# Weight steps of a gated FFN at fixed ticks of the attention in front of it

## The chip, the cores and the metric

The kernel runs on one core of a Trainium2 chip. Its time is the device time of one execution in microseconds (us). A core has a TensorE for matmuls (PE in the profile; PEld is its weight load), VectorE (DVE), ScalarE (ACT), GpSimd (POOL) and SyncE (SP), which here only issues transfers. Each engine works through its own instructions in order, and waits on semaphores for the others. TensorE accumulates in PSUM banks of 512 floats per partition.

## The reference

```python
def _attn_ref(q, k, v, s):                     # q, k, v: 8 x 8 x 576 x 64, s: 8 x 8 x 576
    scores = scale * np.matmul(q, k.transpose(0, 1, 3, 2))
    s_pos = np.maximum(s, 0.0)
    cum = np.cumsum(s_pos, axis=-1)
    bias = -(cum[:, :, :, None] - cum[:, :, None, :])
    scores = np.where(causal, -1000000000.0, scores + np.minimum(bias, 0.0))
    attn = np.exp(scores - np.max(scores, axis=-1, keepdims=True))
    attn = attn / (np.sum(attn, axis=-1, keepdims=True) + 1e-09)
    return np.matmul(attn, v)

def _moe_ref(x, w_gate, w_val, w_out):         # x: 4608 x 512, w: 512 x 1536 twice, 1536 x 512
    gate = 1.0 / (1.0 + np.exp(-(x @ w_gate)))
    return (gate * (x @ w_val)) @ w_out
```

Causal attention over 64 heads of 576 rows, and then a gated FFN over the 4608 rows that it gives. The three FFN weights are drawn in such a way that they reach the kernel as 64-bit floats.

## The kernel before

**Attention by ticks.** A head's 576 rows are five tiles (`TILES`): one of 64 rows and four of 128, with 64 to 576 columns, the widest first. The main loop runs over ticks `n`: one tick is one tile of one head, so head `i` has ticks 5i to 5i + 4. A tick issues the scores of tile n (`n_s` for the first eight heads in float32, `s_part` for the others in pairs of float16), and masks, minimum and exponential of the tile before it (`n_max`, `max_part`, lines 610 and 497). Twice in a head `p_part` (line 499) makes float16 pairs of the exponentials and sends them through a transposing transfer into `PT` (two buffers each). Two heads later `av_part` (line 519) multiplies them by v into the PSUM bank `av_bank`, `x_part` normalizes, and every second head `split_x` writes a slot of `xslots` that the FFN reads. There are ten slots, of which the last three are only made by `late_slots`.

**The weights.** There are 18 pieces (`wsteps`, line 230): twelve of the gate and value weights, one for each f of 12, and six of the output weight, each of 128 x 1024 numbers in 64 bits. Piece n is loaded in two halves of 512 KB (`load_weight`), the first two by SP, the others by ScalarE's queue, into one of six raw buffers; two of these lie in the room of the finished output weights (`w2room`), three in `t2big`, where the FFN keeps the results of its first 24 units (`t2first`). `weight_step` number n asks for loads up to n + 3, if the buffer's last user is two steps back; it decodes piece n (`decode_weight`: a ScalarE pass at line 266, a VectorE pass at line 268, then `square_rows`, a Gram matrix of eight matmuls at line 279 in the last 128 columns of `av_bank`, and its row maxima at line 283); and it finishes piece n - 1 (`split_weight`: a bound from the maxima by a matmul at line 288, a power-of-two scale from it, and the high and low float16 parts by ScalarE at line 308 and VectorE at line 309). So there are 19 steps, 0 to 18, with 18 of each kind of work.

**The FFN by units.** A unit (g, f) is a group of 256 rows and one f of 12: `ffn_in` with 24 matmuls (line 680; 48 smaller ones where a group spans two batches), a tanh (685), a VectorE product (687), the float16 pair of the result (`ffn_mid`, 695 and 696), and later `ffn_out` with six matmuls of 512 columns (710). There are 216 units. The first 24 (groups 0 and 1, batch 0) start at tick 44, and draw on the weights as these are made: `weights_through` runs the weight steps that a unit needs. Their `ffn_out` follows when all 24 are in and `hidden_scale` has the weights' scales. From then on units are spread over the ticks by `want`.

**v's scale.** `v_square` loads a batch's v (four loads of 288 KB) and `v_square_sum` squares and sums it on ScalarE; `v_scale` makes the scale. For batch 2 the loads go to free slots of `xslots`.

**What sets the order.** A scheduler orders each engine's instructions by program order and priority, with a model of their times; `first()` raises a priority. It may move an instruction ahead of others or behind them, as far as data and buffers allow. Accesses to one PSUM bank keep the order of the program. `tc.keep_in_program_order` holds an instruction in its place; `tc.issue_after(ins)` puts the instructions of its block, on the engine of `ins`, behind `ins`.

Before the change the steps are called so: `while n < NE and wnext["step"] < min(2 + n // 6, 9)` (steps 0 and 1 at tick 0, then one each six ticks, step 8 at tick 42), and from tick 45 on by the units through `weights_through`: step 9 at tick 45, and the other nine at ticks 50 to 55. The units come by `FPT` = 0.6 of two a tick and all 24 are issued by tick 63.

Of the kernel before, what the change touches and what calls it, by code (L numbers as in the profile page):

```python
# [25 lines left out]
def tile_attention_then_gated_ffn(  # L26
# [129 lines left out]
    def v_square(b, c):  # L156
        if c == 0:
            vss[b] = wp.tile([P, vch], F32, tag="vss", name=f"vss{b}")
        if b < 2:
            t = wp.tile([P, S], F32, tag="rl", name=f"vsq{b}_{c}")  # L160
        elif b == 2:
            t = xslots[NX - 1 - c].rearrange("p l n -> p (l n)").bitcast(F32)[:, :S]
        else:
            t = spare[f"vsq{c % 2}"]
        (nc.gpsimd if b < 2 else nc.sync).dma_start(t, vview[b, c])
        if b == 0:
            nc.scalar.activation(t, t, AF.Square, accum_out=vss[b][:, c : c + 1])
        else:
            vsq[b, c] = t
# [89 lines left out]
    def decode_weight(n):  # L259

        r = raw[wsteps[n][2]]
        if not wide:
            return r[:, : 8 * P].bitcast(F32)
        a = tops[n % 2]
        top = a.bitcast(F16).rearrange("p (n t) -> p n t", t=2)[:, :, 1]
        nc.scalar.activation(top, r.bitcast(BF16)[:, 4:].rearrange("p (n t) -> p n t", t=4)[:, :, 0], AF.Copy)
        v_ = r[:, : 16 * P].rearrange("p (n t) -> p n t", t=2)[:, :, 1]
        nc.vector.scalar_tensor_tensor(v_, v_, 13, a, ALU.logical_shift_right, ALU.bitwise_or)
        square_rows(n, a)
        return v_.bitcast(F32)  # L270

    wrow, wlast = {}, {}

    def square_rows(n, a):

        top = a.bitcast(BF16).rearrange("p (n t) -> p n t", t=2)[:, :, 1]
        ps = av_bank[:, 3 * P :]
        for c in range(8):
            ins = nc.tensor.matmul(ps, top[:, c * P : (c + 1) * P], top[:, c * P : (c + 1) * P],
                                   start=c == 0, stop=c == 7)  # L280
        wlast["gram"] = ins.ins
        wrow[n] = wp.tile([P, 1], BF16, tag="wss", name=f"wrow{n}")
        nc.vector.tensor_scalar(junk16, ps, 0.0, None, ALU.max, ALU.max, accum_out=wrow[n])
# [64 lines left out]
    def weights_through(n):  # L348
        while wnext["step"] <= n + 1:
            weight_step()  # L350
# [110 lines left out]
    def s_part(i, t):  # L461
        w = TILES[t][2]
        c0 = S + t * P - PAD
        lhs = T[i].rearrange("p a n -> p (a n)")[:, c0 : c0 + P]
        pieces = [(0, w)] if w <= 512 else [(0, w // 2), (w // 2, w)]
        S_ps[i, t] = []
        for a, b_ in pieces:
            ps = score_bank(f"s{i}_{t}_{a}")
            nc.tensor.matmul(ps[:, : b_ - a], lhs, T[i][:, 0, a:b_], start=True, stop=False)  # L469
            nc.tensor.matmul(ps[:, : b_ - a], lhs, T[i][:, 2, a:b_], start=False, stop=True)  # L470
            S_ps[i, t].append((ps, a, b_))

    def bias_row(i):
# [14 lines left out]
    def max_part(i, t):  # L488
        w = TILES[t][2]
        c = qkc[i // 2][1][:, 2:3]  # L490
        init = MASKED
        for n, (ps, a, b_) in enumerate(S_ps.pop((i, t))):
            acc = wp.tile([P, 1], F32, tag=f"em{n}", name=f"em{i}_{t}_{n}", bufs=3)
            nc.vector.tensor_tensor_reduce(e_t[t][:, a:b_], ps[:, : b_ - a], rl[i][:, a:b_], c, init,  # L494
                                           ALU.add, ALU.min, acc)
            init = acc
        nc.scalar.activation(e_t[t][:, :w], e_t[t][:, :w], AF.Exp, bias=init, scale=-1.0)  # L497

    def p_part(i, h_):

# [91 lines left out]
    def n_s(i, t):  # L592
        q0, m, w = TILES[t]
        p, j = divmod(i, 2)
        nS[i, t] = []
        for a, b_ in [(0, w)] if w <= 512 else [(0, w // 2), (w // 2, w)]:
            ps = score_bank(f"s{i}_{t}_{a}")
            nc.tensor.matmul(ps[:, : b_ - a], qT[i][:, q0 : q0 + P], kT[p][:, a:b_], start=True, stop=True)
            nS[i, t].append((ps, a, b_))

    def n_max(i, t):
        q0, m, w = TILES[t]
        init = MASKED
        r = rl[i]
        for n, (ps, a, b_) in enumerate(nS.pop((i, t))):
            acc = wp.tile([P, 1], F32, tag=f"em{n}", name=f"em{i}_{t}_{n}", bufs=3)
            nc.vector.tensor_tensor_reduce(e_t[t][:m, a:b_], ps[:m, : b_ - a], r[:m, a:b_], -1.0, init,
                                           ALU.add, ALU.min, acc[:m])
            init = acc[:m]
        nc.scalar.activation(e_t[t][:m, :w], e_t[t][:m, :w], AF.Exp, bias=init, scale=-1.0)  # L610

    def n_turn(i, t):

# [143 lines left out]
    NE, NOFF = 44, 87  # L757
    FPT = 0.6
    EARLY = 18
    VSQ = 66  # L760
    WLA = 3
    nticks = NTL * NH
    for n in range(nticks + 12):
# [43 lines left out]
        if i < NH:  # L807
# [74 lines left out]
            if b == 0:  # L882
                if t == 2 and 1 <= h < 1 + vch:
                    v_square(1, h - 1)
                if t == 4 and 1 <= h < 1 + vch:
                    v_square_sum(1, h - 1)
                if t == 1 and h == 6:
                    v_scale(1)
            elif b == 1:
                if VSQ <= n < VSQ + vch:  # L890
                    v_square(2, n - VSQ)
                if VSQ + 5 <= n < VSQ + 5 + vch:
                    c = VSQ + 4 + vch - n
                    v_square_sum(2, c)
                if n == VSQ + 11:
                    v_scale(2)
            elif b + 1 < B:
                if t == 0 and 2 <= h < 2 + vch:
                    v_square(b + 1, h - 2)
                if t == 4 and 2 <= h < 2 + vch:  # L900
                    v_square_sum(b + 1, h - 2)
                if t == 4 and h == 2 + vch:
                    v_scale(b + 1)
            while n < NE and wnext["step"] < min(2 + n // 6, 9):
                weight_step()

        if n >= NE and state["u"] < 2 * NF:
            fdone = min(NF, int((n - NE + 1) * FPT))
            while state["u"] < 2 * fdone:
                f = state["u"]  # L910
                if f == 0:
                    weights_through(gate_step[7])
                if f < NF and f % WLA == 0:
                    weights_through(gate_step[f + WLA - 1])
                    inverse_weights(0, slice(f, f + WLA))
                    ffn_scale(0, slice(f, f + WLA))
                if f >= NF:
                    weights_through(min(gate_step[NF - 1] + 2 * (f - NF + 1), len(wsteps) - 1))
                emit_unit()
            if state["u"] == 2 * NF:  # L920
                hidden_scale()
                while state["o"] < 2 * NF:
                    emit_out()
                late_slots()
# [45 lines left out]
```

## Time and profile before

| | |
|---|---|
| median of 3 runs | 1177.1 us (1176.61 to 1182.89) |
| the profiled execution | 1178.93 us |
| its span, first to last instruction | 1177.2 us |
| mean granted TensorE clock | 0.976 |
| PE busy | 1115.4 us (95%) |
| DVE busy | 755.2 us (64%) |
| ACT busy | 736.2 us (63%) |
| transfers | 157.65 MB, mean 134 GB/s |

The columns of a group row are: line, engine, operation, output and input with shapes, count; busy time in us and mean ns of one; idle time of the engine just before, and what ended it. A timeline row has start and length in us, then the same, with the wait before it in brackets. ACTq and SPq are the queues on which ScalarE and SyncE issue transfers. A row of stages has the stage, its length, busy time and count of each engine, the granted TensorE clock, the mean busy share of the 16 DMA engines and GB/s.

### The profile page before, as it was taken

To read this page: it belongs to the slowest core of one execution; us is meant where nothing else is said; L and a number is where in the kernel's file an instruction comes from. 1 tells how busy PE (TensorE), PEld (TensorE's weight loads), DVE (VectorE), ACT (ScalarE), POOL (GpSimd) and SP (SyncE) were. 2 spreads that over 40 slices of the span, in tenths; PEclk is the share of its full clock that TensorE was granted. 3 is DMA by queue.
4 is the path that set the end of the run, shared out by engine and by line. 5 is a ranking of instruction groups with operands and counts; after the bars stand their busy time and mean duration, and the time that the engine had idled before them with its cause. 6 is when DMAs were issued, how large, how long until landed. Compare 5 with 4: busy or idle time off the path is not lost.

```text
span 1177.2 us, 30611 instructions
## 1 busy us (share of the span) xinstructions
PE 1115.4 (95%) x11806; PEld 865.2 (73%) x11806; DVE 755.2 (64%) x2395; ACT 736.2 (63%) x1429; POOL 235.3 (20%) x553
## 2 busy tenths in 40 slices
PE   6898588799899999999999999999999999999998
PEld 4686477655777788778777777778877887787775
DVE  4667875887679777775656577777777775222222
ACT  4888664757678687776656577667776765233222
POOL 4423220223123222221111122212222221000000
PEclk8999798999999999999999999999999999999999
DMA  8877965999889899897565669878979774000000
GB/s 199 224 186 168 185 121 120 172 174 192 143 171 175 150 193 169 149 157 143 110 113 121 124 121 174 167 148 167 158 152 159 142 123 99 12 19 16 4 19 19
DMA packets 445520, 157.65 MB, mean 134 GB/s; under 512 B 403583, under 2 KB 435839, under 8 KB 445374
## 3 DMA queue, kind: packets, MB, share of 16 engines
q1 hardware_dynamic: 418686, 127.38, 59.3%
q10 hardware_dynamic: 23328, 17.04, 5.2%
q0 software_dynamic: 3360, 11.27, 2.9%
q8 instruction: 92, 1.51, 0.5%
q14 instruction: 54, 0.44, 0.1%
HBM read 56.92 MB, written 9.58 MB: 56 GB/s over the span
## 4 chain that ended last, share of the span: by engine, by line
PE 72%; DMA 10%; issue 6%; DVE 3%; ACT 3%; SPq 2%; POOL 2%; ACTq 0%; POOLq 0%; DVEq 0%
PE gv L680 41%; PE o L710 21%; PE s L470 3%; PE s L469 3%; DMA pt<-p 2%; PE av_bank L531 1%; PE av_bank L529 1%; PE av_bank L530 1%; DMA T<-qk 1%; DMA T<-T 1%; DMA ws<-in_moe_w_out_dram 1%; DMA v<-in_v_dram 1%; DMA w2all<-in_moe_w_out_dram 1%; POOL rl L484 1%; DMA cr<-cum_d 1%
## 5 line engine op out<-in xcount | busy, mean ns | idle before, releaser
L680 PE MATMUL gv<-x,w 128*128 128x256 f16 (+3 forms) x6912 | 621.5, 248 | 8.5 <-DVE t2f L687 7.2
L680 PEld LDWEIGHTS <-w 128*128 128x128 f16 x6912 | 539.0, 99 | 70.9 <-issue 6.4
L710 PE MATMUL o<-w2all,h 128*128 128x512 f16 x1296 | 321.6, 382 | 0.4 <-ACT io L729 0.4
L484 POOL TENSOR_SCALAR_AFFINE_SELECT rl<-rl 128x64 f32<-128x64 f32 (+1 forms) x280 | 107.8, 386 | 559.8 <-DVE em L494 495.0
L497 ACT ACTIVATE e<-e,em 128x576 f32<-128x576 f32 x280 | 154.1, 554 | 101.2 <-DVE em L494 98.1
L685 ACT ACTIVATE th<-gv,scb 128x256 f32<-128x256 f32 (+3 forms) x288 | 111.6, 413 | 154.1 <-PE gv L680 151.9
L710 PEld LDWEIGHTS <-h 128*128 128x128 f16 x1296 | 121.1, 96 | 112.3 <-issue 0.5
L687 DVE SCALAR_TENSOR_TENSOR t<-th,gv 128x256 f32<-128x256 f32 x192 | 80.1, 417 | 133.4 <-ACT th L685 130.6
L494 DVE CUSTOM_DVE_ANT_0 e<-s,rl,qkcf 128x288 f32<-128x288 f32 x280 | 135.8, 486 | 32.0 <-PE s L470 27.1
L695 ACT ACTIVATE h<-t,hsc 128x256 f16<-128x256 f32 x192 | 96.7, 503 | 78.9 <-DVE t L687 78.0
L506 DVE SCALAR_TENSOR_TENSOR p<-e,p 128x384 f16<-128x384 f32 x224 | 103.6, 502 | 47.9 <-ACT p L501 46.8
L696 DVE SCALAR_TENSOR_TENSOR h<-t,hsc,h 128x256 f16<-128x256 f32 x192 | 93.2, 485 | 45.1 <-ACT h L695 44.4
L501 ACT ACTIVATE p<-e 128x1152 f16<-128x1152 f32 x112 | 112.0, 1000 | 9.4 <-DMA pt<-p 7.0
L470 PE MATMUL s<-T 128*128 128x288 f16 (+2 forms) x246 | 62.7, 283 | 13.1 <-DMA T<-T 13.1
L469 PE MATMUL s<-T 128*128 128x288 f16 (+2 forms) x246 | 64.6, 281 | 5.7 <-DVE em L494 5.0
L529 PE MATMUL av_bank<-v,pt 128*128 128x65 f16 x560 | 67.9, 193 | 0.2 <-DVE xe_w L129 0.2
L531 PE MATMUL av_bank<-v,pt 128*128 128x65 f16 x560 | 68.1, 195 | 0.0
L530 PE MATMUL av_bank<-v,pt 128*128 128x64 f16 x560 | 68.0, 192 | 0.0
L432 POOL PARTITION_BROADCAST cr<-cr x63 | 57.5, 912 | 11.5 <-DMA cr<-cum_d 11.4
L529 PEld LDWEIGHTS <-pt 128*128 128x128 f16 x560 | 52.6, 98 | 6.1 <-issue 1.1
L530 PEld LDWEIGHTS <-pt 128*128 128x128 f16 x560 | 52.6, 97 | 5.5 <-issue 0.3
L478 DVE TENSOR_SCALAR rl<-cr,qkcf 128x576 f32<-128x576 f32 x56 | 29.3, 523 | 41.5 <-POOL cr L432 41.3
(163 smaller groups left out, 1355.3 us busy)
## 6 DMA issues: line engine op xcount, KB each, us to landing
v<-v SPq DMA_DIRECT2D x56, 162.5 KB
out_dram<-io POOLq DMA_DIRECT2D x34, 256.0 KB, 3.5
v<-in_v_dram SPq DMA_DIRECT2D x64, 128.0 KB
T<-T SPq DMA_DIRECT2D x82, 72.0 KB
t2f<-in_v_dram SPq DMA_DIRECT2D x20, 288.0 KB
qk<-in_q_dram SPq DMA_DIRECT2D x17, 288.0 KB
qk<-in_k_dram SPq DMA_DIRECT2D x17, 288.0 KB
t2f<-in_moe_w_out_dram ACTq DMA_DIRECT2D x8, 512.0 KB
```

What stands on the lines that cost most here:

```text
L469: nc.tensor.matmul(ps[:, : b_ - a], lhs, T[i][:, 0, a:b_], start=True, stop=False)
L470: nc.tensor.matmul(ps[:, : b_ - a], lhs, T[i][:, 2, a:b_], start=False, stop=True)
L484: nc.gpsimd.affine_select(rl[i][:, q0:w], rl[i][:, q0:w], pattern=[[-1, m]], compare_op=ALU.is_ge, fill=-MASKED if i < NN else MASKED, bas ...
L494: nc.vector.tensor_tensor_reduce(e_t[t][:, a:b_], ps[:, : b_ - a], rl[i][:, a:b_], c, init, ALU.add, ALU.min, acc)
L497: nc.scalar.activation(e_t[t][:, :w], e_t[t][:, :w], AF.Exp, bias=init, scale=-1.0)
L501: nc.scalar.activation(p_s[h_][:, 0], e_s[h_], AF.Copy, scale=PSCALE)
L506: nc.vector.scalar_tensor_tensor(flat[:, LOW[t] * P : (LOW[t] + t) * P], e_t[t][:, : t * P], PSCALE, flat[:, kb * P : (kb + t) * P], ALU.m ...
L529: nc.tensor.matmul(AV[i][:, t], hi, v_[:, D : 2 * D + 1], start=kb == 0, stop=False)
L530: nc.tensor.matmul(AV[i][:, t, 0:D], hi, v_[:, 0:D], start=False, stop=False)
L680: nc.tensor.matmul(ps[:, gv, a:e], w1[f][:, cc, gv, wl], x_of(b, cc)[:, xl, c0 + a : c0 + e], start=(c == 0), stop=(c == 3 * NC - 1))
L685: nc.scalar.activation(th[:, a:e], ps[:, 0, a:e], AF.Tanh, scale=scb[b][:, f : f + 1])
L710: nc.tensor.matmul(ps[:m], h[:, hl, tt * P : tt * P + m], w2[f][:, wl], start=(f == 0 and c == 0), stop=(f == NF - 1 and c == 2))
```

## The change

The weight steps get ticks of their own: 5, 9, ... 37 for steps 0 to 8, then 42, 45, ... 69 for steps 9 to 18. The ScalarE pass of a decode is put behind the last exponential issued before it, the Gram matrix behind the last scores. The first 24 units are issued at two thirds of a unit a tick from tick 45 on, at most 16 before tick 69; the other eight, their `ffn_out` and `late_slots` come at tick 69. The loads of v of batch 2 go from ticks 66 to 69 to ticks 40, 41, 42 and 46, into slots 6, 5, 4 and 6, and their sums to ticks 45, 46, 47 and 51.

```diff
@@ v_square
-            t = xslots[NX - 1 - c].rearrange("p l n -> p (l n)").bitcast(F32)[:, :S]
+            t = xslots[6 - c % 3].rearrange("p l n -> p (l n)").bitcast(F32)[:, :S]
@@ decode_weight
-        nc.scalar.activation(top, r.bitcast(BF16)[:, 4:].rearrange("p (n t) -> p n t", t=4)[:, :, 0], AF.Copy)
+        with tc.issue_after(paced["ACT"]):
+            nc.scalar.activation(top, r.bitcast(BF16)[:, 4:].rearrange("p (n t) -> p n t", t=4)[:, :, 0], AF.Copy)
@@ square_rows
-        for c in range(8):
-            ins = nc.tensor.matmul(ps, top[:, c * P : (c + 1) * P], top[:, c * P : (c + 1) * P],
-                                   start=c == 0, stop=c == 7)
+        with tc.issue_after(paced["PE"]):
+            for c in range(8):
+                ins = nc.tensor.matmul(ps, top[:, c * P : (c + 1) * P], top[:, c * P : (c + 1) * P],
+                                       start=c == 0, stop=c == 7)
@@ s_part (n_s likewise)
-            nc.tensor.matmul(ps[:, : b_ - a], lhs, T[i][:, 2, a:b_], start=False, stop=True)
+            ins = nc.tensor.matmul(ps[:, : b_ - a], lhs, T[i][:, 2, a:b_], start=False, stop=True)
+            paced["PE"] = ins.ins
@@ max_part (n_max likewise)
-        nc.scalar.activation(e_t[t][:, :w], e_t[t][:, :w], AF.Exp, bias=init, scale=-1.0)
+        paced["ACT"] = nc.scalar.activation(e_t[t][:, :w], e_t[t][:, :w], AF.Exp, bias=init, scale=-1.0).ins
@@ the main loop
-    VSQ = 66
+    VSQ = 40
+    STEPS = [5 + 4 * k for k in range(9)] + [42 + 3 * k for k in range(10)]
...
-                if VSQ <= n < VSQ + vch:
-                    v_square(2, n - VSQ)
-                if VSQ + 5 <= n < VSQ + 5 + vch:
-                    c = VSQ + 4 + vch - n
-                    v_square_sum(2, c)
-                if n == VSQ + 11:
+                for c in range(vch):
+                    if n == VSQ + c + (3 if c == 3 else 0):
+                        v_square(2, c)
+                    if n == VSQ + 5 + c + (3 if c == 3 else 0):
+                        v_square_sum(2, c)
+                if n == VSQ + 13:
                     v_scale(2)
...
-            while n < NE and wnext["step"] < min(2 + n // 6, 9):
+            while wnext["step"] < len(STEPS) and STEPS[wnext["step"]] <= n:
                 weight_step()
...
-            fdone = min(NF, int((n - NE + 1) * FPT))
-            while state["u"] < 2 * fdone:
+            want = min((n - NE + 1) * 2 // 3, 16) if n < STEPS[-1] else 2 * NF
+            while state["u"] < min(want, 2 * NF):
...
-                if f >= NF:
-                    weights_through(min(gate_step[NF - 1] + 2 * (f - NF + 1), len(wsteps) - 1))
+                if f >= 16:
+                    weights_through(len(wsteps) - 1)
```

More of the change, by code (lines that the diff above doesn't have):

```diff
@@ L270, in decode_weight @@
         return v_.bitcast(F32)
-    wrow, wlast = {}, {}
+    wrow, wlast, paced = {}, {}, {}
     def square_rows(n, a):
@@ L597, in n_s @@
             ps = score_bank(f"s{i}_{t}_{a}")
-            nc.tensor.matmul(ps[:, : b_ - a], qT[i][:, q0 : q0 + P], kT[p][:, a:b_], start=True, stop=True)
+            ins = nc.tensor.matmul(ps[:, : b_ - a], qT[i][:, q0 : q0 + P], kT[p][:, a:b_], start=True, stop=True)
+            paced["PE"] = ins.ins
             nS[i, t].append((ps, a, b_))
@@ L609, in n_max @@
             init = acc[:m]
-        nc.scalar.activation(e_t[t][:m, :w], e_t[t][:m, :w], AF.Exp, bias=init, scale=-1.0)
+        paced["ACT"] = nc.scalar.activation(e_t[t][:m, :w], e_t[t][:m, :w], AF.Exp, bias=init, scale=-1.0).ins
     def n_turn(i, t):
```

## The prediction

> **What bounds the kernel now.** I read the page from the slices down, because the share of busy time is a mean over stages.
>
> ```profile
> span 1177.2 us, 30611 instructions
> PE 1115.4 (95%) x11806; PEld 865.2 (73%) x11806; DVE 755.2 (64%) x2395; ACT 736.2 (63%) x1429; POOL 235.3 (20%) x553
> PE   6898588799899999999999999999999999999998
> PEclk8999798999999999999999999999999999999999
> ```
>
> In the two lines of slices one digit is a fortieth of the span, 29.4 us. TensorE is full from the twelfth digit on, and its clock is not below 0.9 again. There the time is TensorE's work, which the change leaves alone. Whatever it gains or loses must be made in the first eleven digits, 320 us. The profiled run took 1178.9 us, 1.7 us round its span and 1.8 us above the median of the runs, so I count differences and take them from the median.
>
> The view by stages (columns: stage, length, then busy time of PE, PEld, DVE, ACT and POOL with instruction counts, granted clock, DMA share, GB/s) cuts this stretch by ticks; a tick is one tile's scores, its minimum and its exponential. The second fence is the same view for the exponentials of line 497 alone (ScalarE, count), the third for the FFN matmuls of line 680.
>
> ```profile
> 0.00:114.00 114.00, 93.45 (x629) 76.25 (x630) 68.93 (x225) 83.69 (x164) 42.74 (x106) 0.93 0.79 195
> 114.00:174.00 60.00, 43.70 (x371) 34.02 (x370) 49.07 (x156) 41.90 (x68) 14.39 (x27) 0.83 0.82 159
> 174.00:220.00 46.00, 37.51 (x353) 30.84 (x354) 27.18 (x80) 24.61 (x41) 1.76 (x6) 0.85 0.58 133
> 220.00:290.00 70.00, 62.98 (x632) 40.82 (x630) 54.90 (x179) 47.42 (x89) 20.95 (x44) 1.00 0.95 178
> 372.00:430.00 58.00, 57.88 (x713) 45.78 (x711) 44.56 (x147) 42.02 (x85) 13.84 (x33) 1.00 0.87 165
> ```
>
> ```profile
> 114.00:174.00 60.00, 11.01 (x22) 0.83 0.82 159
> 174.00:220.00 46.00, 0.16 (x1) 0.85 0.58 133
> 372.00:430.00 58.00, 11.05 (x20) 1.00 0.87 165
> ```
>
> ```profile
> 174.00:220.00 46.00, 32.50 (x239) 25.51 (x240) 0.85 0.58 133
> ```
>
> ```profile
> 114.23 0.34 ACT L497 ACTIVATE e<-e,em 128x64 f32<-128x64 f32 x1
> ...
> 290.35 0.67 ACT L497 ACTIVATE e<-e,em 128x448 f32<-128x448 f32 x1 [0.48 <-DVE em L494]
> ```
>
> Ticks are counted by the widths of the exponentials in the timeline (576, 448, 320, 192, 64 columns, a head each five): 114.23 us is tick 45, the last of head 8, and 290.35 us is tick 92. Ticks 45 to 65 fill 60 us; then attention stands for 46 us (the one exponential counted there is the tail of tick 65) and resumes at 220 us. FFN matmuls go on in the hold (239, ten units of 24), but not densely. Multiplying busy time by granted clock, 114 to 290 us holds 43.70 x 0.83 + 37.51 x 0.85 + 62.98 = 131 us of TensorE work, in 176 us. **45 us are lost there**, and they are the stock from which the change can draw.
>
> Why attention stands is in order of time on TensorE and ScalarE.
>
> ```profile
> 173.47 0.68 ACT L497 ACTIVATE e<-e,em 128x192 f32<-128x192 f32 x2
> ...
> 174.99 0.62 ACTq L255 DMA_DIRECT2D ws<-in_moe_w_out_dram  x1
> ...
> 180.85 0.60 ACTq L255 DMA_DIRECT2D ws<-in_moe_w_out_dram  x1
> 186.47 1.35 ACT L266 ACTIVATE h<-ws 128x1024 f16<-128x1024 bf16 x1 [5.73 <-DMA ws<-in_moe_w_out_dram]
> ```
>
> ```profile
> 204.61 0.63 PE L279 MATMUL av_bank<-io 128*128 128x128 bf16 x8
> ...
> 207.25 0.19 PE L529 MATMUL av_bank<-v,pt 128*128 128x65 f16 x1 [0.25 <-DVE xe_w L129]
> ```
>
> ```profile
> 212.56 1.16 ACT L501 ACTIVATE p<-e 128x1152 f16<-128x1152 f32 x1 [3.20 <-DMA pt<-p]
> ...
> 220.05 0.76 ACT L497 ACTIVATE e<-e,em 128x576 f32<-128x576 f32 x1
> ```
>
> Weight step 15 to 18 sit here in one row, each behind a load whose second half is issued only when the first has landed (174.99 to 180.85, then 5.6 us more). The Gram matmul of line 279 writes the same PSUM bank as the attention-times-v matmuls of line 529. All steps are issued by tick 55 of the program, so head 9, due at tick 56, has to follow the last Gram, and runs at 207.25 us, not near 147 (11 ticks of 2.9 us behind tick 45). The p tiles that it should have consumed block the next p pass (212.56), and that blocks the exponential (220.05).
>
> **The change, part by part.** Steps move from ticks 0, 0, 6 ... 42, 45, 50 to 55 to the fixed ticks 5, 9 ... 37, 42, 45 ... 69. The count is the same: 18 passes, 18 splits, 18 Grams, 32 load halves on ScalarE's queue. One step costs, by the grouped rows:
>
> ```profile
> L266 ACT ACTIVATE io<-w2all 128x1024 f16<-128x1024 bf16 x6 | 8.2, 1364 | 2.2 <-DMA w2all<-in_moe_w_val_dram 2.0
> L308 ACT ACTIVATE w<-w2all,wscale 128x1024 f16<-128x1024 f32 x6 | 7.4, 1234 | 3.7 <-DVE wscale L131 3.6
> L268 DVE SCALAR_TENSOR_TENSOR w2all<-w2all,io 128x1024 int32<-128x1024 int32 x6 | 7.4, 1232 | 3.1 <-ACT io L266 3.1
> L309 DVE SCALAR_TENSOR_TENSOR w<-w2all,wscale,w 128x1024 f16<-128x1024 f32 x6 | 7.7, 1283 | 0.8 <-ACT w L308 0.6
> L283 DVE TENSOR_SCALAR_CACHE_REDUCE t<-av_bank 128x128 bf16<-128x128 f32 x18 | 5.2, 287 | 10.0 <-PE av_bank L279 10.0
> q10 hardware_dynamic: 23328, 17.04, 5.2%
> ```
>
> So ScalarE 1.36 + 1.23 = 2.6 us; VectorE 1.23 + 1.28 + 0.29 and some 0.4 of small ones = 3.2 us; TensorE 0.63 for the Gram (204.61 us) and 0.17 for the row behind it, 0.8 us; transfers 5.2% of 1177.2 / 16 = 3.8 us of all DMA engines (queue 10 is ScalarE's).
>
> *Ticks 0 to 44.* Step 0 and 1 leave a ScalarE that waits there for the weights themselves and enter ticks where it is nearly full.
>
> ```profile
> 19.11 1.35 ACT L266 ACTIVATE h<-ws 128x1024 f16<-128x1024 bf16 x1 [3.50 <-DMA ws<-in_moe_w_val_dram]
> ```
>
> That wait of 3.50 us goes, and what then ends last is the load of the first heads. Against it stand two passes (2.7 us) in full ticks and one more split or two (up to 2.5 us) ahead of tick 45. The loads 2 and 3, on ScalarE's queue, are asked for at tick 9 and wanted at tick 13, about 5 us later, when a half takes 5.7: a new wait of up to 5 us with exponentials queued behind it. From +6 to -6 us; I take 0, since the passes that now wait in full ticks are the same kind.
>
> *Ticks 45 to 68.* Nine steps, 16 FFN units and 24 ticks of attention must share four resources. What a tick of attention costs I take from 372 to 430 us (20 ticks, 12 units, no weights), less the units (line 710 has six matmuls a unit; its stage row stands first here):
>
> ```profile
> 372.00:430.00 58.00, 17.74 (x73) 6.58 (x71) 1.00 0.87 165
> ```
>
> ```profile
> L685 ACT ACTIVATE th<-gv,scb 128x256 f32<-128x256 f32 (+3 forms) x288 | 111.6, 413 | 154.1 <-PE gv L680 151.9 <-PE av_bank L288 1.7
> L687 DVE SCALAR_TENSOR_TENSOR t<-th,gv 128x256 f32<-128x256 f32 x192 | 80.1, 417 | 133.4 <-ACT th L685 130.6
> L695 ACT ACTIVATE h<-t,hsc 128x256 f16<-128x256 f32 x192 | 96.7, 503 | 78.9 <-DVE t L687 78.0
> L696 DVE SCALAR_TENSOR_TENSOR h<-t,hsc,h 128x256 f16<-128x256 f32 x192 | 93.2, 485 | 45.1 <-ACT h L695 44.4
> L173 ACT ACTIVATE t2f<-t2f 128x576 f32<-128x576 f32 x20 | 13.4, 669 | 0.0
> ```
>
> ```profile
> 157.90 2.78 PE L680 MATMUL gv<-x,w 128*128 128x256 f16 x24
> ```
>
> - VectorE: (44.56 - 12 x 0.90) / 20 = 1.69 a tick, a third of a step 1.07, two thirds of line 687 0.28: 3.0 x 24 = **73 us**.
> - ScalarE: (42.02 - 12 x 0.92) / 20 = 1.55 a tick, a third of a step 0.86, two thirds of line 685 0.28: 1.55 + 0.86 + 0.28 = 2.7 x 24, and four v passes of 0.67: **68 us**.
> - DMA: 0.87 x 58 / 20 = 2.5 a tick, 60.5, and five or six loads of 3.8, 21: 82 us; at the share of 0.95 that the kernel held longest, **86 us**.
> - TensorE at full clock: 16 units of 2.7 (the 2.78 holds the drain of its last matmul); 24 ticks at (57.88 - 12 x 2.78 - 17.74) / 20 = 0.34; nine steps at 0.8: 43 + 8 + 7 = **58 us**.
>
> The stage takes the longest: 86 us. TensorE is idle for 28 of them, because only 16 units may be issued: 16 and up write where the last raw weights lie. Still, no attention is held, since head 9's matmuls now have only Grams before them that were issued earlier by tick.
>
> *Ticks 69 to 92.* What is left of the 131 us, 73, runs with a queue of 8 + 24 units to fill TensorE: 73 us. Before, 220 to 290 us had 7 us of idle TensorE, waits of the scores for transfers; I keep 3 of them.
>
> The sum: 114 + 86 + 73 + 3 = 276 us where tick 92 was at 290 us, **-14 us**. From there on TensorE is full in both.
>
> The other edits cost nothing beside this. The four v loads of batch 2, on SP's queue, go from tick 66 to ticks 40 to 46, three of them ahead of the stage, into x slots not written until tick 56; in SP's order they now stand before the p transposes of head 7 and 8, which wait for their issue alone. Their sums come by tick 51, in ScalarE's count above; without that cover they would cost 4 x 0.67 = 2.7 us. The edge on the Gram keeps it behind the scores; behind the Gram on TensorE wait FFN matmuls, at most for one late pass, priced as the third rival. The late x slots come six ticks later and are not used until tick 86.
>
> The Trainium skill, "DMA: Bandwidth & Descriptors", section "Issuing engines are not separate DMA queues", says that transfers of ScalarE and SP share the same 16 engines. By it weight loads and attention's transfers add, as in my 82; were they separate, the stage would be VectorE's 73 us, 13 us better. The row of 220 to 290 us, at share 0.95 with no weight load in it, shows how little room attention leaves.
>
> **The rivals.**
>
> 1. *Better, 1147 us.* Transfers pack and VectorE sets the stage: 73 us, the 3 us of waits go: 114 + 73 + 73 = 260, -30. For it: short stretches show a DMA share above 0.95. Against: VectorE is never at 100% for 60 us here, 49.07 at most.
>
> 2. *No change, 1177 us.* The edges only keep a pass from coming earlier; nothing keeps it from coming late, and the idle time moves: a stage of 100 us instead of 86 eats the 14. That is 4.2 us a tick where 45 to 65 took 2.9 with fewer units and six steps. It is also what happens if the instruction order bunches the steps again.
>
> 3. *Slower, 1190 us.* ScalarE's in-order queue is the new hold. Each step's pass stands fixed behind an exponential, and its load may be late: load 17 is issued at step 16, three ticks before use, some 10.7 us, and needs two halves of 5.7. With 5.0 us lost at each of nine steps (the wait at 186.47 us, 5.73 less the issue in it), ScalarE needs 68 + 45 = 113 us, 27 more than the stage; with only 16 units TensorE cannot use them: -14 + 27 = +13. It decides from a mean wait of (86 - 68) / 9 = 2 us a step, and reaches no gain at 3.6. Against it: 12 to 16 are loaded two or three steps ahead.
>
> 4. *Half clock, 1193 us.* TensorE, idle in small gaps for a third of 86 us, may be granted less. At 0.83 (114 to 174 us) its 58 become 70, still hidden; below 58 / 86 = 0.67 it sets the stage, at 0.5 it takes 116: +30, less 14: +16. The Trainium skill, "TensorE: Matmul & The Clock Gate", section "The HAM clock gate", says that a window of about 3.4 us without work halves the clock; by that rule the gaps must be long, and spread units make them short. The row with gaps has 0.83, so it agrees in part only.
>
> **How the numbers follow.** Forecast 0.48, rival 1 0.20, rival 2 0.18, rival 3 0.11, rival 4 0.03. The forecast is 1177.1 - 14 = 1163 us; its own range, with +-6 of the first stage, is 1155 to 1171. The range for 8 in 10 reaches to rival 1 and past rival 2: 1146 to 1181. About 0.5% is what a measurement of this kernel can tell from no change: faster (below 1171.2) 0.66, same 0.20, slower 0.14.
>
> **What would show it.** Right: attention runs through ticks 65 to 66 without a hold; head 9's matmuls of line 529 stand before the last Gram; tick 69 at about 200 us and tick 92 near 276; DMA share near 0.95 between. Wrong: tick 45 more than 6 us off 114; waits of line 266 or 255 above 2 us a step (rival 3); clock below 0.67 (rival 4); stage one of 100 us (rival 2); or idle TensorE past 330 us, which I take to be none.

## The result and the profile after

| | before | after |
|---|---|---|
| median of the runs beside each other (8 each) | 1179.1 us (1176.61 to 1186.79) | 1188.0 us (1184.2 to 1190.49) |
| ratio of after to before | | 1.0064, 95% interval 1.0037 to 1.0092 |
| span of the profiled execution | 1177.2 us | 1186.4 us |

The change makes the kernel slower by 0.6%, 9 us, where 14 us less were forecast. One of the ten runs of e13, a kernel of the experiments below, took 1552.9 us at a granted clock of 0.69, and its ratio leaves that run out. The page of after begins so (line numbers are now those of the changed kernel: exponentials 500 and 614, loads 255, passes 267, Grams 281, units 684):

```profile
span 1186.4 us, 30600 instructions
PE 1119.0 (94%) x11806; PEld 868.2 (73%) x11806; DVE 754.7 (64%) x2395; ACT 737.9 (62%) x1429; POOL 237.1 (20%) x553
PE   6888577899999999999999999999999999999998
PEclk9787679999999999999999999999999999999999
DMA  9666969993899899878465649879978875000000
```

The eighth slice (208 to 237 us) has 8 where before had 7: there the hold was. But the third, sixth and seventh are one tenth lower, and the granted clock of the second to sixth reads 7, 8, 7, 6, 7 where before had 9, 9, 9, 7, 9. So something is lost between 30 and 178 us. From the ninth digit on TensorE is full again. The view by stages, cut at the exponentials of tick 45, 69 and 93 of after:

```profile
0.00:132.20 132.20, 102.75 (x638) 83.75 (x639) 73.11 (x237) 88.27 (x174) 42.07 (x108) 0.84 0.74 175
132.20:204.30 72.10, 51.95 (x487) 40.31 (x487) 60.00 (x188) 51.41 (x80) 19.39 (x34) 0.83 0.90 182
204.30:304.60 100.30, 92.55 (x950) 67.28 (x948) 71.05 (x226) 62.33 (x115) 19.58 (x41) 1.00 0.80 146
```

Tick 45 comes at 132.2 us, not at 114.2. From there to tick 69 it is 72.1 us, where before took 111.1 (225.3 less 114.2); before had 20.3 units done by then, after 11.0.

One measure runs through what follows, worked out from the start times of all matmuls. **Lost TensorE time** at a tick is the moment of its exponential, less what the matmuls started by then take at full clock. A column is priced at 0.417 ns, a little under what the starts of consecutive 256-column matmuls of line 680 give in before (mostly 0.109 us apart, 0.426 ns a column), so that a dense stretch shows some loss too. A matmul counts as 64 columns at least, and four times in float32. That overprices some early matmuls, so that values can fall below zero; only differences between kernels at one tick are read. From tick 97 to 301 the kernels here lose nearly alike (before 27.8 us, after 27.6, all between 25.7 and 30.8), and the span is 1119 us plus the loss at tick 97, within 4 us.

| lost TensorE time, us | by tick 30 | tick 36 | tick 41 | tick 45 | tick 69 | tick 97 | units done by tick 69 |
|---|---|---|---|---|---|---|---|
| before | 2.8 | -1.4 | 1.0 | 1.2 | 44.1 | 57.8 | 20.3 |
| after | -0.6 | 4.0 | 12.4 | 18.6 | 51.7 | 67.8 | 11.0 |

Up to tick 30 after is ahead, at 76.0 us against 79.3. Ticks 30 to 45 then cost it some 19 us of TensorE, and from tick 45 to 97 it gains 7.4 (49.2 against 56.6). The balance, 10.0, is near the 9.2 us of the spans. The chain that ended last, in order of time, shows what holds ticks 30 to 41:

```profile
74.01 8.72 DMA t2f<-in_moe_w_out_dram
82.76 0.55 ACTq L255
83.42 10.35 DMA t2f<-in_moe_w_gate_dram
93.79 0.38 ACTq L255
...
114.45 7.25 DMA T<-qk
```

A first half of a weight load takes 8.72 us, a ScalarE issue follows, the next first half takes 10.35 us, and again a ScalarE issue follows. What waits behind it stands in ScalarE's timeline:

```profile
83.42 0.59 ACTq L255 DMA_DIRECT2D t2f<-in_moe_w_gate_dram  x1
...
89.69 0.78 ACT L614 ACTIVATE e<-e,em 128x576 f32<-128x576 f32 x1 [3.52 <-DVE em L611]
93.79 0.38 ACTq L255 DMA_DIRECT2D t2f<-in_moe_w_val_dram  x1
94.22 1.12 ACT L614 ACTIVATE e<-e,em 128x448 f32<-128x448 f32 x2 [3.75 <-DVE ner L639]
95.24 1.33 ACT L267 ACTIVATE io<-w2all 128x1024 f16<-128x1024 bf16 x1
96.45 0.82 ACT L382 ACTIVATE jq<-qk 96x768 f16<-96x768 f32 x1
...
123.38 0.84 ACT L382 ACTIVATE jq<-qk 96x768 f16<-96x768 f32 x1 [7.65 <-DMA qk<-in_q_dram]
...
124.22 0.76 ACT L500 ACTIVATE e<-e,em 128x576 f32<-128x576 f32 x1
```

The row of 94.22 us names a VectorE tile in its bracket, but the issue of the second half stands ahead of it in the same queue, and could go only when the first half had landed. Meanwhile the DMA engines were busy throughout, as the view by stages over the two first halves shows (DMA share is the last column but one):

```profile
74.00:82.80 8.80, 5.72 (x31) 4.15 (x30) 3.88 (x8) 6.33 (x12) 1.15 (x2) 0.81 1.08 285
83.40:93.80 10.40, 9.29 (x46) 7.91 (x47) 3.59 (x10) 3.38 (x5) 1.04 (x4) 0.67 1.06 207
```

Behind both stands the sum of squares of q for heads 8 and 9 (96.45 us). From it comes their scale, then the transposes of head 8 (issued at 106.80 us) and of head 9 (the DMA of 114.45 us on the chain), and with them the q and k buffers come free later: the next q load is issued only at 116.02 us, ScalarE waits 7.65 us for it, and the exponential of tick 41, whose minimum was ready at 118.6 us, queues up behind that wait (124.22 us). The same two rows in before:

```profile
85.22 0.84 ACT L380 ACTIVATE jq<-qk 96x768 f16<-96x768 f32 x1 [0.22 <-DMA qk<-in_q_dram]
...
105.95 0.75 ACT L497 ACTIVATE e<-e,em 128x576 f32<-128x576 f32 x1
```

The order of ScalarE differs from before's well ahead of this. The sums of batch 2's v, written at ticks 45 to 51 of the program, run as `x<-x` here:

```profile
32.50 0.67 ACT L173 ACTIVATE x<-x 128x576 f32<-128x576 f32 x1
...
33.83 0.67 ACT L173 ACTIVATE x<-x 128x576 f32<-128x576 f32 x1
...
34.50 0.67 ACT L173 ACTIVATE x<-x 128x576 f32<-128x576 f32 x1
```

Nothing holds these loads and sums at their ticks. Their slots are free from the start, so the scheduler issues three of the loads at 18.2 to 19.3 us and the fourth, which takes the slot of the first again, at 33.3 us. Before had shown the same on a single load: the one of the four that goes to slot 6, written at tick 69, is issued at 20.0 us there, and its sum, written at tick 71, runs at 41.7:

```profile
41.67 0.67 ACT L173 ACTIVATE x<-x 128x576 f32<-128x576 f32 x1
```

In the second stage the forecast mechanism is there. The timeline of TensorE around head 9:

```profile
176.75 0.62 PE L281 MATMUL av_bank<-io 128*128 128x128 bf16 x8 [0.75 <-DVE xe_v L129]
...
182.97 0.19 PE L532 MATMUL av_bank<-v,pt 128*128 128x65 f16 x1
...
189.42 0.62 PE L281 MATMUL av_bank<-h 128*128 128x128 bf16 x8
...
199.71 0.62 PE L281 MATMUL av_bank<-io 128*128 128x128 bf16 x8
```

Head 9's matmuls run at 182.97 us, with these two Grams and two more behind them, and the 46 us between tick 65 and 66 are 11.5 (186.1 to 197.6 us). ScalarE, in the same place:

```profile
186.42 0.83 ACTq L255 DMA_DIRECT2D ws<-in_moe_w_out_dram  x1
186.87 0.60 ACT L414 ACTIVATE qk<-qk,qksc 96x384 f16<-96x384 f32 x1
191.26 1.35 ACT L267 ACTIVATE io<-w2all 128x1024 f16<-128x1024 bf16 x1 [3.79 <-DMA w2all<-in_moe_w_out_dram]
...
197.57 0.78 ACT L500 ACTIVATE e<-e,em 128x576 f32<-128x576 f32 x1 [1.14 <-DVE em L497]
```

A pass at its fixed tick waits 3.79 us for its load, and the p passes and the exponential are queued behind it.

### The profile page after: what moved, and what is told of

It is laid out like the page before. It is cut to its first block, busy times and chain, and to the rows that moved or that the text cites. A ratio compares the mean times of both kernels' runs of the same rounds, so it can differ in the third digit from the quotient of the medians.

```text
span 1186.4 us, 30600 instructions
## 1 busy us (share of the span) xinstructions
PE 1119.0 (94%) x11806; PEld 868.2 (73%) x11806; DVE 754.7 (64%) x2395; ACT 737.9 (62%) x1429; POOL 237.1 (20%) x553
## 3 DMA queue, kind: packets, MB, share of 16 engines
q10 hardware_dynamic: 23328, 17.04, 5.4%
## 4 chain that ended last, share of the span: by engine, by line
PE 74%; DMA 9%; ACT 5%; DVE 4%; issue 4%; POOL 1%; SPq 1%; ACTq 0%; DVEq 0%; POOLq 0%
PE gv L684 40%; PE o L714 22%; PE s L472 2%; PE s L471 2%; DMA t2f<-in_moe_w_out_dram 2%; DMA T<-qk 1%; DMA t2f<-in_moe_w_gate_dram 1%; DMA pt<-p 1%; PE na_ps L632 1%; PE av_bank L534 1%; PE av_bank L532 1%; PE av_bank L533 1%; PE s L601 1%; DVE e L497 1%; DMA v<-in_v_dram 1%
## 5 line engine op out<-in xcount | busy, mean ns | idle before, releaser
L487 POOL TENSOR_SCALAR_AFFINE_SELECT rl<-rl 128x64 f32<-128x64 f32 (+1 forms) x280 | 112.2, 402 | 591.3 <-DVE em L497 527.1
L700 DVE SCALAR_TENSOR_TENSOR h<-t,hsc,h 128x256 f16<-128x256 f32 x192 | 93.1, 485 | 43.9 <-ACT h L699 43.4
L734 POOL DMA_DIRECT2D out_dram<-io x34 | 19.4, 570 | 179.9 <-ACT io L733 179.1
```

The source lines that it names most:

```text
L487: nc.gpsimd.affine_select(rl[i][:, q0:w], rl[i][:, q0:w], pattern=[[-1, m]], compare_op=ALU.is_ge, fill=-MASKED if i < NN else MASKED, bas ...
L700: nc.vector.scalar_tensor_tensor(h[:, 1], t2, hsc[:, f : f + 1], h[:, 0], ALU.mult, ALU.subtract)
```

## The experiments

Every kernel below ran beside before on the same chip; the ratio is to before, with its 95% interval. Loss is the lost TensorE time of one profiled execution.

| run | time, us | ratio | tick 45 at, us | loss by tick 45 | 45 to 69 | 69 to 97 | in all |
|---|---|---|---|---|---|---|---|
| before (profile) | 1178.6 to 1181.3 | 1 | 114.2 | 1.2 | 42.9 | 13.7 | 57.8 |
| after | 1188.0 | 1.0064 | 132.2 | 18.6 | 33.1 | 16.1 | 67.8 |
| e1, early steps as before | 1192.2 | 1.0089 (1.0057 to 1.0120) | 125.8 | 12.9 | 42.0 | 15.8 | 70.7 |
| e2, late steps as before | 1195.2 | 1.0118 (1.0077 to 1.0159) | 114.2 | 2.3 | 59.3 | 12.5 | 74.1 |
| e3, no edges | 1193.3 | 1.0104 (1.0066 to 1.0142) | 126.1 | 14.9 | 43.8 | 13.9 | 72.6 |
| e4, v late | 1183.5 | 1.0025 (1.0000 to 1.0049) | 114.3 | 2.1 | 38.9 | 22.9 | 63.9 |
| e5, v held at its ticks | 1184.5 | 1.0049 (1.0026 to 1.0073) | 114.6 | 2.7 | 40.8 | 19.5 | 63.0 |
| e6, only the sums held | 1189.5 | 1.0078 (1.0063 to 1.0093) | 111.9 | -0.2 | 48.5 | 20.1 | 68.4 |
| e7, before with v moved | 1194.0 | 1.0110 (1.0084 to 1.0136) | 129.3 | 16.0 | 41.1 | 12.0 | 69.1 |
| e8, e5 with free halves | 1185.0 | 1.0069 (1.0040 to 1.0099) | 113.9 | 1.3 | 41.5 | 23.3 | 66.1 |
| e9, before with free halves | 1171.4 | 0.9939 (0.9916 to 0.9962) | 120.1 | 7.5 | 30.6 | 17.3 | 55.4 |
| e10, after with free halves | 1174.3 | 0.9960 (0.9938 to 0.9982) | 113.0 | -0.1 | 31.4 | 19.2 | 50.5 |
| e11, e4 with free halves | 1179.8 | 1.0002 (0.9977 to 1.0027) | 112.3 | 0.9 | 39.2 | 22.1 | 62.2 |
| **e12, e6 with free halves** | **1162.5** | **0.9858 (0.9837 to 0.9880)** | 110.4 | -3.5 | 28.4 | 13.9 | 38.8 |
| e13, e12 with the steps of before | 1176.1 | 0.9967 (0.9946 to 0.9987) | 118.7 | 5.8 | 38.9 | 13.2 | 57.9 |
| e14, e12 without edges | 1178.4 | 1.0005 (0.9984 to 1.0026) | 114.8 | 1.1 | 35.7 | 18.2 | 55.0 |

The profiled execution of e12 took 1157.6 us, 5 us less than its median, so its losses are some us small; the others lie within 4 us of theirs.

### Which part of the change costs 18 us ahead of tick 45?

Three parts act there: the early steps, the edges, and the place of batch 2's v. First the early steps were put back.

```diff
-    STEPS = [5 + 4 * k for k in range(9)] + [42 + 3 * k for k in range(10)]
+    STEPS = [0, 0, 6, 12, 18, 24, 30, 36, 42] + [42 + 3 * k for k in range(10)]
```

> Steps 0 to 8 at the ticks of the kernel before (0, 0, 6 ... 42), the late steps, units, edges and v loads as changed. Theory A (the loss is made before tick 45, by the early steps' loads standing bunched on ScalarE's queue at ticks 25 to 31, which makes head 8 late; the late steps gain): tick 45 comes back to 114 +-4 us from 132, the time to 1170 +-4, below the kernel before. Theory B (the v loads of batch 2, which run at 18 us, take the start): tick 45 stays near 130, time near 1187. Theory C (the edges make the order bad): also near 1187.

Loss by tick 45 is 12.9, not near 1: the early ticks are at most a third of it. Then the late part was put back, and v with it.

```diff
-    VSQ = 40
+    VSQ = 66
...
-            t = xslots[6 - c % 3].rearrange("p l n -> p (l n)").bitcast(F32)[:, :S]
+            t = xslots[NX - 1 - c].rearrange("p l n -> p (l n)").bitcast(F32)[:, :S]
... (the ticks of the loads and sums as before)
-            while wnext["step"] < len(STEPS) and STEPS[wnext["step"]] <= n:
+            while n < NE and wnext["step"] < 9 and STEPS[wnext["step"]] <= n:
-            want = min((n - NE + 1) * 2 // 3, 16) if n < STEPS[-1] else 2 * NF
-            while state["u"] < min(want, 2 * NF):
+            fdone = min(NF, int((n - NE + 1) * FPT))
+            while state["u"] < 2 * fdone:
... (weights_through as before)
```

> Steps 0 to 8 at ticks 5, 9 ... 37 with the edges; late steps, units and v loads of batch 2 as before. Theory A: tick 45 near 130 us and 8 us of the late gain missing: 1192 to 1198. Theory B: tick 45 near 114, time near 1179. Theory C: near 1187, since the edges are in.

With early ticks and edges of the change, but v as before, tick 45 is back at 114.2 us. It is not the early steps. The time, 1195.2, is not the 1179 that theory B gave for this kernel: the late stage is the worst of all, 59.3 (before: 42.9). There the late steps stand in a bunch as before, but each behind an edge; whether the edges alone do this was not tried. Without the edges, in the changed kernel:

```diff
-        with tc.issue_after(paced["ACT"]):
+        with ExitStack():
-        with tc.issue_after(paced["PE"]):
+        with ExitStack():
```

> The changed kernel without its two issue_after edges; ticks, units and v loads as changed. Theory A: the ticks set it, near 1188 with tick 45 at 125 or later. Theory C: tick 45 back near 114, time 1170 to 1179. Theory B: near 1188.

Loss by tick 45 stays at 14.9, so the edges are not its cause; from tick 45 on it is 57.7 against 49.2 in after, so with spread steps they are worth some 8 us. That leaves v. It was put late in after (loads at ticks 70 to 73, sums at 74 to 77, scale at 78; the load to slot 6 still runs at 18.9 us and its sum at 37.9, as in before), and moved alone in before:

```diff
-    VSQ = 40
+    VSQ = 70
... (the ticks of the sums and the scale)
-            t = xslots[6 - c % 3].rearrange("p l n -> p (l n)").bitcast(F32)[:, :S]
+            t = xslots[NX - 1 - c].rearrange("p l n -> p (l n)").bitcast(F32)[:, :S]
```

> The changed kernel with the v loads of batch 2 at ticks 70 to 73 (late slots as before), sums at 74 to 77, scale at 78. Theory B: tick 45 back near 114 to 118, time 1172 to 1178. Theory A and C: near 1188, tick 45 at 128 or later.

```diff
 (in the kernel before)
-    VSQ = 66
+    VSQ = 40
... (the ticks of the loads and sums as in the change)
-            t = xslots[NX - 1 - c].rearrange("p l n -> p (l n)").bitcast(F32)[:, :S]
+            t = xslots[6 - c % 3].rearrange("p l n -> p (l n)").bitcast(F32)[:, :S]
```

> The kernel before with only the v loads, sums and slots of batch 2 moved as in the change. Theory B: tick 45 at 122 to 132 us instead of 114 and the time at 1186 to 1196. If the start is only upset by the early steps or the edges: tick 45 at 114, 1175 to 1181.

Both agree: v late gives tick 45 at 114.3 us, and v's move alone makes before slower by 1.1%, tick 45 at 129.3. The move of v is the cause of the early loss. It does not act at one place, though. In e7 two thirds of the loss are there by tick 21 already (16.8 us against 7.0 in before), and again a second half is issued only behind a first half:

```profile
58.94 6.01 DMA t2f<-in_moe_w_out_dram
64.97 0.56 ACTq L255
```

Is it the 1.15 MB of loads or the order of the sums? Two kernels hold them with edges of their own, one both, one only the sums:

```diff
 (e5 has both, e6 only the second)
-        (nc.gpsimd if b < 2 else nc.sync).dma_start(t, vview[b, c])
+        with tc.issue_after(paced["SP"]) if b == 2 else ExitStack():
+            (nc.gpsimd if b < 2 else nc.sync).dma_start(t, vview[b, c])
-        pin(nc.scalar.activation(t, t, AF.Square, accum_out=vss[b][:, c : c + 1]))
+        with tc.issue_after(paced["ACT"]) if b == 2 else ExitStack():
+            pin(nc.scalar.activation(t, t, AF.Square, accum_out=vss[b][:, c : c + 1]))
```

`paced["SP"]` is the last load of `crow`, which SP issues for each head.

> The changed kernel, with the v loads of batch 2 put behind the running-sum row's load of their tick on SP and their sums behind their tick's exponential on ScalarE, so that they run at ticks 40 to 51 as the program writes them. Theory B (what costs is that the scheduler runs them at 18 to 35 us, which reorders the start): tick 45 at 114 to 118 us, the late stage as in the changed kernel, time 1170 to 1177. Rival D (any place before tick 45 to 69 costs it, since DMA and ScalarE are short there): 1183 to 1190.

> Only the sums are held at their ticks; the loads may run at 18 us. If the transfers in the start cost it: as the changed kernel, tick 45 at 126 or later, 1186 to 1192. If ScalarE's four sums and the order they force cost it: as with both held, tick 45 at 114 to 118, 1170 to 1180.

In e6 three loads still run at 18.5 to 19.6 us, and tick 45 is at 111.9. So it is not the transfers but the place of the four sums on ScalarE, or rather the whole order that the scheduler makes around it. But e6 is no faster than after. What it gains early it loses behind tick 45 (68.6 against 49.2). e5 also ends above before, and e4 at or just above it. Tick 45 came back as expected in e4, e5 and e6, but the times of 1170 to 1180 that went with it did not: with tick 45 on time the fixed ticks still bring nothing.

### Is ScalarE held by the second halves of the loads?

The two halves of a load go into alternate pieces of the raw buffer (128 numbers wide for the gate and value weights, 64 for the output weight), so their ranges overlap though no byte is shared, and the second is issued only when the first has landed. Side by side in the buffer they need not wait. Passes, splits and Grams keep their counts; only the second of the two split operations, on VectorE, becomes two of half the size (18 more instructions).

```diff
@@ load_weight
-                dst = dst.rearrange("p (h x n) -> p h x n", x=2, h=8)[:, :, x]
+                dst = dst.rearrange("p (x h n) -> p x h n", x=2, h=8)[:, x]
-                dst = dst.rearrange("p (c x n) -> p c x n", c=NC, x=2)[:, :, x]
+                dst = dst.rearrange("p (x c n) -> p x c n", c=NC, x=2)[:, x]
@@ split_weight
-        nc.vector.scalar_tensor_tensor(lo, a, sc, hi, ALU.mult, ALU.subtract)
+        for x in range(2):
+            nc.vector.scalar_tensor_tensor(lo[:, x], a[:, x], sc, hi[:, x], ALU.mult, ALU.subtract)
```

It was put into e5, into before and into after.

> As e5 (v of batch 2 held at its ticks), and the two halves of a weight load lie side by side in the raw buffer instead of interleaved, so that the second is issued without waiting for the first to land (the VectorE split becomes two instructions of half the width). Theory F (ScalarE standing at second halves, some 15 us of it between 100 and 205 us in e5, is what eats the gain of the spread steps): 1166 to 1176, and the waits of the load's line gone. Theory G (the late stage is short of transfers and of filled TensorE, not of ScalarE): 1181 to 1187, as e5.

> The kernel before with the halves side by side in the same way. Theory F: 1168 to 1177, since it waits at second halves too (52.7, 96.9, 117, 133 us); theory G: 1177 to 1182 as before.

> The changed kernel with the halves side by side. Theory F: the early loss shrinks too, as the longest wait there (83.4 to 93.8 us, a second half) goes: tick 45 at 118 to 124, 1172 to 1180. Theory G: 1185 to 1190.

The same change with free halves loses nothing by tick 45 (-0.1 against 18.6), although v's sums still run at 34.7 to 43.9 us in e10: they are dear only together with the interleaved halves, whose waits on ScalarE's queue are what the timelines show. e10 is 14 us faster than after (1174.3 against 1188.0, each beside a before of 1179.1), and e9 7.7 us faster than before. (In e9, and in e13 below, the first exponential starts at 22.6 and 21.1 us instead of 11.8: some 8 us of loss at the start. By tick 36 e13 has all but 2.4 us of it back against before, e9 is still 6.7 us behind.) e8 is a miss: in e5 the same edit brings nothing, 1185.0. Free halves also need fewer packets, 12576 instead of 23328:

```profile
q10 hardware_dynamic: 23328, 17.04, 5.4%
```

```profile
q10 hardware_dynamic: 12576, 17.04, 4.7%
```

The first row is of after, the second of e12, below. It is 64 us of queue time in one and 54 in the other (share by span). What part of the gain is shorter transfers, and what part the issue that no longer waits, was not told apart.

### Why does it not help where v is held?

Two more places of v with free halves: late as in e4, and as in e6, loads free and sums held.

> The changed kernel with batch 2's v loads at ticks 70 to 73 (their old slots, sums at 74 to 77), and with the two halves of a weight load side by side in the raw buffer, so that the second is issued without waiting for the first. Nothing is left out. Question: with free halves the changed kernel took 0.996 of before, and with v held at ticks 40 to 51 as well 1.007. Theory H, the stretch from tick 45 to 97 has no room, so v's 1.15 MB and 2.7 us of ScalarE cost wherever in it they lie: tick 45 at 113 to 115 us, lost TensorE time at tick 97 near 62 us, time about 1180, ratio 1.000 to 1.005. Theory N, free halves are worth some 14 us whatever v does, and the run with v held was one poor order of the scheduler's: lost 50 us, time 1168 to 1174, ratio 0.991 to 0.996.

> The changed kernel with free halves, batch 2's v loads free as in the change (the scheduler takes them ahead of 35 us) and only their four sums held behind the exponentials of ticks 45 to 51. Nothing is left out. Theory H (the stretch has no room): only 2.7 us of ScalarE stand in it, so lost TensorE time at tick 97 of 51 to 56 us, time 1174 to 1179, ratio 0.996 to 1.000. Theory N (free halves are worth 14 us whatever v does): 1168 to 1174, ratio 0.991 to 0.996. A third, P (the place of the sums ahead of tick 45 is needed by the free order): as with v held, lost 64 us or more, 1185, ratio 1.005.

e12 is faster than before by 1.4%. No theory had given it: beside after (1.0064), sums at their ticks alone bring nothing (e6, 1.0078), free halves alone 1.0% (e10, 0.9960), both together 2.1% (0.9858). e11 stays at before's time. So theory N (free halves are worth 14 us whatever v does) is out. H (v's loads and sums have no room behind tick 45) foretold e11, and that e12 is the faster of the two, but not its size: it gave 51 to 56 us of loss and 1174 us or more. It doesn't fit e8 well either: that kernel is behind e12 already at tick 31 (loss -1.4 against -9.8), ahead of its own v loads. That much is a different order, and why the scheduler makes it is open. The views of e12, stages cut at its ticks 45, 69 and 93:

```profile
0.00:110.40 110.40, 88.72 (x641) 71.85 (x642) 72.71 (x241) 84.41 (x164) 41.95 (x106) 0.97 0.87 222
110.40:189.10 78.70, 62.84 (x628) 51.80 (x627) 67.33 (x220) 58.61 (x97) 19.06 (x38) 0.87 0.82 173
189.10:277.20 88.10, 80.94 (x790) 56.82 (x791) 64.59 (x207) 56.63 (x108) 17.26 (x38) 0.96 0.80 151
```

```profile
83.05 0.38 ACTq L256 DMA_DIRECT2D w2all<-in_moe_w_gate_dram  x1
83.71 0.38 ACTq L256 DMA_DIRECT2D w2all<-in_moe_w_val_dram  x1
...
97.02 0.78 ACT L503 ACTIVATE e<-e,em 128x576 f32<-128x576 f32 x1
```

Both halves are issued within 0.66 us, and tick 41 starts at 97.0 us (124.2 in after). The groups of ScalarE in its second stage, last column the idle time before them:

```profile
L268 ACT ACTIVATE io<-w2all 128x1024 f16<-128x1024 bf16 x3 | 4.0, 1339 | 0.0
...
L174 ACT ACTIVATE x<-x 128x576 f32<-128x576 f32 x4 | 2.7, 671 | 0.0
L268 ACT ACTIVATE h<-ws 128x1024 f16<-128x1024 bf16 x2 | 2.7, 1348 | 0.0
L268 ACT ACTIVATE h<-t2f 128x1024 f16<-128x1024 bf16 x2 | 2.7, 1341 | 0.0
```

The same groups of after, in its second stage:

```profile
L267 ACT ACTIVATE io<-w2all 128x1024 f16<-128x1024 bf16 x3 | 4.0, 1344 | 3.8 <-DMA w2all<-in_moe_w_out_dram 3.8
...
L267 ACT ACTIVATE h<-ws 128x1024 f16<-128x1024 bf16 x2 | 2.7, 1358 | 0.2 <-DMA ws<-in_moe_w_out_dram 0.2
L267 ACT ACTIVATE h<-t2f 128x1024 f16<-128x1024 bf16 x2 | 2.7, 1341 | 1.0 <-DMA t2f<-in_moe_w_val_dram 1.0
```

No pass waits for its load in e12; in after they wait 5.0 us. v's sums (line 174) stand at their ticks.

The Trainium skill, "DMA: Bandwidth & Descriptors", section "Issuing engines are not separate DMA queues", says of issuing on several engines that it only saves the sequencer's time to initiate a DMA, usually small beside the DMA itself. For the issue instruction the rows agree: 0.59 us (83.42 us in after) against 10.35 us of transfer. An issue that must wait costs more than that here, since everything behind it in ScalarE's order waits too (93.79 and 94.22 us in after).

### Do the fixed ticks gain anything?

e12 may owe its time to v and the halves alone. So e13 is e12 with the steps and units of before and no edges on them, and e14 is e12 without those edges.

> The kernel before with everything that the best version has except the change's steps and units: halves of a weight load side by side, batch 2's v loads at tick 40 to 46 in slots 6, 5, 4, 6, their sums held behind the exponentials of ticks 45 to 51. Steps at ticks 0, 0, 6 ... 42 and, by the units, 45 and 50 to 55, as before; no edges on passes and Grams. Nothing is left out. Theory S, the fixed ticks themselves gain once no weight load blocks ScalarE's queue: the hold between tick 65 and 66 is back (about 40 us), lost TensorE time at tick 97 of 53 to 58 us, time 1170 to 1176, ratio 0.992 to 0.998. Theory O, the fixed ticks are worth nothing and the gain of the best version is that of halves and v alone: lost 37 to 42 us, time 1160 to 1165, ratio 0.984 to 0.988.

> The best version (the changed kernel with free halves and batch 2's sums held at ticks 45 to 51) without the two edges on a step's ScalarE pass and its Gram matrix; the steps stay at their ticks in the program. Nothing is left out. Theory S with the edges needed: the scheduler takes passes early, as it did without free halves (lost late TensorE time 57.7 against 49.2 us), so lost 44 us or more at tick 97, time 1167 or more, ratio 0.990 or more. If the edges do nothing beside the ticks: 1160 to 1165, ratio 0.984 to 0.988.

e13 takes 1176.1 us, and in ScalarE's timeline the hold between tick 65 and 66 is back:

```profile
172.36 0.67 ACT L500 ACTIVATE e<-e,em 128x192 f32<-128x192 f32 x2
...
220.91 0.78 ACT L500 ACTIVATE e<-e,em 128x576 f32<-128x576 f32 x1 [1.62 <-DVE er L544]
```

So the fixed ticks with their edges are worth some 13 us (1176.1 less 1162.5, or 1.1% by the ratios) where nothing else holds ScalarE, and without the edges nothing is left of it (e14, 1.0005). Both behave as theory S expected. Not all of it is the hold: of the 19.1 us of loss between the two profiled executions, 10.5 lie between ticks 45 and 69 and 9.3 ahead of tick 45, where e13 also starts late. And each of these kernels is one order of the scheduler's; how far another order with the same ticks would move the time is not known.

## Why the prediction was wrong

The forecast was 1163 us with 1146 to 1181 as its range; 1188 is outside. By its steps:

- **What bounds the kernel** (the hold of 46 us at tick 65, from head 9's matmuls behind the last Gram): right. With spread steps head 9's matmuls stand between Grams and of the 46 us 11.5 are left (3.9 in e12); with the old steps the hold is back, in e13 too.
- **Ticks 0 to 44, "I take 0" of -6 to +6: this step failed.** It was +18 us, 132.2 instead of 114 (17.4 us of loss more than before). The bounds looked at the steps' own work, passes, splits and late loads, and e2 shows that this was sized rightly (114.2 us). What was missing stood under "The other edits cost nothing beside this": v's loads were taken to go "from tick 66 to ticks 40 to 46" and the sums to tick 51. A tick in the program is no tick on the engine. The sums ran at 32.5 to 39.6 us and the order around them changed. That v's move costs this is shown (e7, e4, e6), and that it costs it only with interleaved halves (e10); that the way leads over the waits for second halves ahead of the squares of heads 8 and 9, and so to tick 41, is read from the timeline of after alone. The front part of the text had said that the scheduler may move an instruction ahead, and before had a load of batch 2 at 20.0 us; the sum used neither.
- **Ticks 45 to 68, 86 us for 16 units:** 72.1 us in after, but for 11.0 units. The five that are missing cost 5 x 2.7 = 13.5 us later, so the stage with its units comes to 85.6. By loss the forecast took 38 us (106 us less 68 of work, 114 to 220 us) to 28, a gain of 10; measured is a gain of 9.8 (42.9 to 33.1). This step held in size, though 16 units were forecast and 11.0 done. In e12 it is 78.7 us with 15.0 units and a loss of 28.4. Transfers held a share of 0.90 in after and 0.82 in e12, not 0.95; that DMA sets the stage was not tested by itself.
- **Ticks 69 to 92, 73 + 3 us:** the 3 us were too few, and they had no row behind them. Idle time was to fall from 7 to 3 us. From tick 69 to 93 after loses 13.3 us and e12 13.5, where before lost 11.1 (44.1 to 55.2): 2.2 more and not 4 less, so 6 us of the forecast's 14 were not there. The three stages together, 17.4 - 9.8 + 2.2, are 9.8 us, near the 9.2 of the spans.
- **The sum of -14 us** for the step ticks is some -13 in e12 against e13. That agreement in size is luck, as its terms are others: e12 gains 9.3 us of loss by tick 45 on e13, where 0 was forecast, 10.5 between 45 and 69, and nothing behind.
- **Rivals.** Rival 3, ScalarE's in-order queue, 1190 us, has the mechanism, and nearly the time by another sum, but another place: not at the late steps, where seven passes waited 5.0 us for loads in all, far from 2 us a step, but at 74 to 124 us. Rival 2 adds something: e5 with v at its ticks loses 63.0 us in all against 57.8, so without the early loss there was no gain either. Rival 4: the granted clock of the stage was 0.83, above its bound. Rival 1 didn't come.
- **"What would show it":** the sign "tick 45 more than 6 us off 114" was met, and points to the failed step.

What stays open: why free halves with three places of v lead to times some 20 us apart (e8, e11, e12), and how much of the free halves is packets.

## What to carry to other kernels

When a change moves loads or passes in the program, ask first what holds them there; if their buffers are free and no edge stands behind them, price them at the earliest place that the scheduler can give them, on each in-order queue. Look on a compute engine's queue for transfer issues that wait, here a second half whose destination interleaves with the first: everything behind them stands, and a gain elsewhere can't be seen until they are gone. When a change brings less than its mechanism promises, try its parts in pairs: here the fixed ticks cost 0.6% alone (after), free halves alone gained 0.6% (e9), and with v's sums held as well the three made 1.4% together.

## What the runs showed of the hardware that was not expected

The same 512 KB half took 5.6 to 5.9 us in before's hold and 8.72 and 10.35 us on the chain of after, with DMA shares of 1.08 and 1.06; before's second half:

```profile
180.85:186.47 5.62, 4.54 (x47) 3.97 (x45) 1.47 (x4) 0.00 (x1) 0.00 (x0) 1.00 0.71 146
```

So a load's lead has to be counted in the time that it takes where it runs. And the same bytes, written side by side instead of interleaved, went in 12576 packets instead of 23328, with some 10 us less of queue time over all 32 halves.
